# Turning the keys and the probabilities of a decode attention on VectorE instead of TensorE

## The chip, the cores and the metric

The kernel runs on one core of a Trainium2 chip. The metric is the device time of one execution in microseconds (us), as the median of several runs. A core has TensorE (PE), whose matmuls read SBUF and write PSUM; VectorE (DVE), ScalarE (ACT) and GpSimd (POOL); SyncE (SP), which here issues nearly all the transfers; and 16 DMA engines that carry them. Each engine works through its own instructions in order and waits on semaphores for the others.

## The reference

One token `x` of 576 values goes through two branches, which a gate mixes:

```
q = (x @ wq)                       # 32 query heads of 128, wq is 576 x 4096
k, v = the last 4096 positions of the caches of 16 key heads, two query heads share one
p = softmax(q k^T / sqrt(128));  a = (p v) @ wo        # wo is 4096 x 576
h = gelu(x @ w1 + b1);           b = h @ w2 + b2       # w1 576 x 4608, w2 4608 x 576
g = sigmoid(sum(x * gate_w));    out = g * a + (1 - g) * b
```

All tensors are bf16. Keys and values are 16.8 MB each, the four weight matrices 20.1 MB together; every byte is used once, 53.6 MB in all.

## The kernel before

The 16 key heads are taken four at a time (`HT`), so there are four key tiles and four value tiles (`NT`), each 128 partitions of 32 KB, 4.19 MB. Partition `p` of a tile belongs to head `p // 32` of the four and holds 128 consecutive positions of 128 values (`load_kv`, L104). The pool `kv_pool` has three buffers that keys, values and at the end `w2` pass through in turn; `w_pool` has two for `wq`, `w1` and `wo`. All these loads are issued by SP, in the order of the program text, and a load waits until the last reader of its buffer is done; what stands behind it on SP waits too. The order of the transfers is: first quarter of `wq`, k0, the rest of `wq`, k1, k2, v0, the first half of `w1`, k3, the second half of `w1`, v1, v2, v3, `wo` in two halves, `w2` in eight pieces.

The schedule is manual: on every engine the instructions run in the order in which the text issues them, and the framework adds the waits.

Scores need the keys with their 128 values on the partitions. `transposes(h, i)` (L276) makes four matmuls of 128x128 with `perm`, a permuted identity, as moving operand (L281), into one PSUM tile `tp`, and then copies it to `kT` as bf16, three of eight on DVE (L290), five on ACT (L292). `UT` is 4, so a key tile is worked in four units of eight such steps; `kT_pool` has four buffers.

`scores(h, s)` (L302) makes four matmuls of 32 columns of output partitions each, which PE runs side by side (L311). `qz` holds the queries between zeros; a window into it (`lo`) places two query columns at the row pair that belongs to the unit, so that the scores of two tiles gather in one PSUM bank `s_ps`, batch by batch (`TB` is 2, `NB` is 2).

`softmax(b)` (L319) copies the scores to SBUF, takes row maxima, turns these on PE to one row, joins the rows of a head, spreads the result back and takes the exponential on ACT with the sum accumulated (L355). `put(n)` (L363), four for each batch, turns the probabilities on PE (L367), and DVE multiplies them with a mask into `ez` (L374). `values(h, i)` (L391) multiplies `ez` with the value tile, 32 matmuls a tile in four column groups (L400), and `heads_out(t)` (L414) adds up the four masked blocks on DVE and turns the result on PE (L430).

`w1_mul` (L498) is the first layer of the other branch, `gelu` (L517) adds the bias, turns `h` with nine steps on PE (L538) and evaluates the gelu into `gt`. `gate` (L580) and `norm` (L598) make the mixing factor and the softmax scale. At the end `ow` (L733), the scaled attention in column form, is multiplied with `wo` in blocks of four rows (L759), the same loop goes on over the first rows of `w2`, and `part_s` (L766) gathers these sums. The last rows of `w2` are added in `row_matmul` (L776), then the result is copied and stored.

The main loop (L633) interleaves these: for each unit of keys the eight steps of the next unit, the two score steps, one step of the softmax `chain`, later the value matmuls of the first tile and the first layer. After it the value matmuls of the second tile stand between the steps of the second softmax, and the nine turns of `h` between its `put`s.

Of the kernel before, what the change touches and what calls it, by code (L numbers as in the profile page):

```python
# [16 lines left out]
def kernel(  # L17
# [28 lines left out]
    UT = 4  # L46
    NCH = NCK // UT
    NU = NT * UT
    F = 4608
# [22 lines left out]
    NBL = NCH // BC  # L72
    NBK = 2 * UT
    CB = NCK // NBK
    QZ = 2 * (TB * NBK - 1)

# [3 lines left out]
    w_pool = ctx.enter_context(tc.tile_pool(name="w_pool", bufs=2))  # L80
    const = ctx.enter_context(tc.tile_pool(name="const", bufs=1))
    kT_pool = ctx.enter_context(tc.tile_pool(name="kT_pool", bufs=4))
    small = ctx.enter_context(tc.tile_pool(name="small", bufs=1))
    ps_t = ctx.enter_context(tc.tile_pool(name="ps_t", bufs=3, space=bass.MemoryType.PSUM))
    ps_s = ctx.enter_context(tc.tile_pool(name="ps_s", bufs=1, space=bass.MemoryType.PSUM))
    ps_m = ctx.enter_context(tc.tile_pool(name="ps_m", bufs=1, space=bass.MemoryType.PSUM))
    ps_o = ctx.enter_context(tc.tile_pool(name="ps_o", bufs=1, space=bass.MemoryType.PSUM))
# [30 lines left out]
    WMAX = 41 * 256  # L118

    def load_flat(src, lo, n, name, cuts=(), between=None):  # L120
        t = w_pool.tile([P, WMAX], BF16, name=name, tag="w")
        edges = (0, *cuts, n)
        for i, (a, b) in enumerate(zip(edges, edges[1:])):
            if i == 1 and between is not None:
                between()
            nc.sync.dma_start(out=t[:, a:b], in_=src[:, lo + a : lo + b])  # L126
        return t
# [15 lines left out]
    def first_keys():  # L143
# [5 lines left out]
    QP = 2 * NM  # L149
    wq_t = [  # L150
        load_flat(wq_flat, 0, QP * QC, "wq_t", (NQ * QC,), first_keys),
        load_flat(wq_flat, QP * QC, QP * QC, "wq_t"),
    ]

# [17 lines left out]
    qz = const.tile([P, Hkv, QZ + 34], BF16, name="qz")  # L172
# [45 lines left out]
    for t in range(TB):  # L218
        nc.vector.tensor_reduce(
            out=m_b[:, t, 0:R].rearrange("p (g q) -> p g q", q=2),  # L220
            in_=ident_f[:].rearrange("p (g t b q) -> p t g q b", g=HT, t=TB, q=2)[:, t],
            axis=AX.X,
            op=ALU.add,
        )
    nc.vector.tensor_scalar(
        out=m_b[:].rearrange("p t x -> p (t x)"), in0=m_b[:].rearrange("p t x -> p (t x)"),
        scalar1=1.0 / HT, scalar2=None, op0=ALU.mult,
    )
    own = const.tile([P, HT], FP32, name="own")
    nc.vector.tensor_reduce(  # L230
        out=own[:], in_=ident_f[:].rearrange("p (i g) -> p g i", g=HT), axis=AX.X, op=ALU.add
    )
    own_r = const.tile([P, R], FP32, name="own_r")
    nc.vector.tensor_copy(
        out=own_r[:].rearrange("p (g q) -> p g q", q=2),
        in_=own[:].rearrange("p (g o) -> p g o", o=1).to_broadcast([P, HT, 2]),
    )
    perm = const.tile([P, P], BF16, name="perm")
    nc.vector.tensor_copy(
        out=perm[:].rearrange("p (g i) -> p g i", g=HT),  # L240
        in_=ident[:].rearrange("p (i g) -> p g i", g=HT),
    )
    pick = const.tile([P, TB * NBK, HT, 2], BF16, name="pick")
    nc.vector.tensor_copy(
        out=pick[:], in_=ident[:].rearrange("p (g x q) -> p x g q", g=HT, q=2)
# [30 lines left out]
    def transposes(h, i):  # L276
        if i == 0:
            kT[h] = kT_pool.tile([P, W], BF16, name="kT", tag="kT")
        tp = ps_t.tile([P, BC * P], FP32, name="tp", tag="tp")
        for c in range(BC):  # L280
            nc.tensor.matmul(  # L281
                tp[:, c * P : (c + 1) * P],
                lhsT=k_tiles[h // UT][:, (h % UT) * NCH + i * BC + c, :],
                rhs=perm[:],
                start=True,
                stop=True,
            )
        dst = kT[h][:, i * BC * P : (i + 1) * BC * P]
        if i in (0, 3, 6):
            nc.vector.tensor_copy(out=dst, in_=tp[:])  # L290
        else:
            nc.scalar.copy(out=dst, in_=tp[:])  # L292


    s_tiles = {}


    NN = CB // BC
    ez = const.tile([P, TB, NBK, NN, BC, R], BF16, name="ez")
    sums = const.tile([P, NB], FP32, name="sums")  # L300

    def scores(h, s):  # L302

        t, b = h // UT, 2 * (h % UT) + s
        row = NBK * (t % TB) + b
        if row == 0:
            s_tiles[t // TB] = ps_s.tile([P, CB, PI], FP32, name="s_ps", tag="s")
        lo = QZ - 2 * row
        kT_v = kT[h][:].rearrange("p (c g i) -> p c g i", g=HT, i=PI)
        for g in range(HT):  # L310
            nc.tensor.matmul(  # L311
                s_tiles[t // TB][32 * g : 32 * (g + 1), :, :],
                lhsT=qz[:, HT * t + g, lo : lo + 32],
                rhs=kT_v[:, s * CB : (s + 1) * CB, g, :],
                start=(row == 0),
                stop=(row == TB * NBK - 1),
            )

    def softmax(b):  # L319
# [3 lines left out]
        ms = small.tile([P, CB, PI], FP32, name="ms", tag="ms")  # L323
        m16 = small.tile([1, HT * TB, 2], FP32, name="m16", tag="m16")
        m_all = small.tile([1, P], FP32, name="m_all", tag="m_all")
        nb = small.tile([P, 1], FP32, name="nb", tag="nb")
        pr = small.tile([P, CB, PI, HT], BF16, name="pr", tag="pr")

        def row_max():
            nc.vector.tensor_copy(out=ms[:], in_=s_ps[:])  # L330
            nc.vector.tensor_reduce(  # L331
                out=mx[:], in_=ms[:].rearrange("p c i -> p (c i)"), axis=AX.X, op=ALU.max
            )

        def turn_max():
            mT = ps_m.tile([1, P], FP32, name="mT", tag="m")
            nc.tensor.transpose(out=mT[:], in_=mx[:], identity=ident_f[:])
            nc.vector.tensor_reduce(
                out=m16[:], in_=mT[:].rearrange("o (a b q) -> o a q b", b=NBK, q=2), axis=AX.X,
                op=ALU.max,  # L340
            )
            nc.vector.tensor_copy(
                out=m_all[:].rearrange("o (a b q) -> o a b q", b=NBK, q=2),
                in_=m16[:].rearrange("o a (b q) -> o a b q", b=1).to_broadcast(
                    [1, HT * TB, NBK, 2]
                ),
            )

        def spread():
            mb = ps_m.tile([P, 1], FP32, name="mb", tag="m")  # L350
            nc.tensor.matmul(mb[:], lhsT=m_all[:], rhs=ones_ff[0:1, 0:1], start=True, stop=True)
            nc.vector.tensor_scalar(  # L352
                out=nb[:], in0=mb[:], scalar1=-SCALE, scalar2=None, op0=ALU.mult
            )
            nc.scalar.activation(  # L355
                out=pr[:].rearrange("p c i g -> p (c i) g"),
                in_=ms[:].rearrange("p c (i g) -> p (c i) g", g=1).to_broadcast(
                    [P, CB * PI, HT]
                ),
                func=ACT.Exp, bias=nb[:, 0:1], scale=SCALE, accum_out=sums[:, b : b + 1],  # L360
            )

        def put(n):  # L363
            pool, tag = (ps_m, "m") if b == 0 else (ps_t, "tp")
# [268 lines left out]
    for h in range(UT - 1, NU):  # L633
# [27 lines left out]
        if h == UT + 2:  # L661
            gate()
# [164 lines left out]
```

## Time and profile before

| what | value |
|---|---|
| median of 3 runs | 134.89 us (134.27 to 136.29) |
| the profiled execution's own time | 133.93 us |
| its span, first to last instruction | 132.1 us |
| mean granted TensorE clock | 0.88 |
| PE, DVE, ACT busy | 90.1, 62.4, 50.3 us |
| DMA queue q1 | 53.62 MB, 95.4% of 16 engines' span |
| instructions | 2599, of them 1121 matmuls |

The profiled execution has about 1.8 us outside its span. Busy time of an engine is the time in which it has an instruction in work; several matmuls can be in work at once, so a group's busy time is less than its count times the mean of one. In groups of instructions a line reads: line of the kernel, engine, operation, output and inputs with shapes, count, then busy us, mean ns of one, and the idle time of the engine ahead of them with what ended it.

### The profile page before, as it was taken

To read this page: it belongs to the slowest core of one execution; us is meant where nothing else is said; L and a number is where in the kernel's file an instruction comes from. 1 tells how busy PE (TensorE), PEld (TensorE's weight loads), DVE (VectorE), ACT (ScalarE), POOL (GpSimd) and SP (SyncE) were. 2 spreads that over 40 slices of the span, in tenths; PEclk is the share of its full clock that TensorE was granted. 3 is DMA by queue.
4 is the path that set the end of the run, shared out by engine and by line. 5 is a ranking of instruction groups with operands and counts; after the bars stand their busy time and mean duration, and the time that the engine had idled before them with its cause. 6 is when DMAs were issued, how large, how long until landed. Compare 5 with 4: busy or idle time off the path is not lost.

```text
span 132.1 us, 2599 instructions
## 1 busy us (share of the span) xinstructions
PE 90.1 (68%) x1121; PEld 59.5 (45%) x1121; DVE 62.4 (47%) x144; ACT 50.3 (38%) x89; POOL 2.9 (2%) x10
## 2 busy tenths in 40 slices
PE   0000578896698879497889998984799655472562
PEld 0000577663465656266655575751496321241241
DVE  2910255662255546836535457487376475400021
ACT  3000256980277777483475646580600000000001
POOL 8000000000000000000000000000000000000000
PEclk9999999999999999955599999999965777779855
DMA  4998999999899999999989999999999899999960
GB/s 112 514 417 387 408 460 441 436 461 440 367 476 451 407 407 426 427 426 466 446 365 439 470 441 387 456 441 407 436 456 432 386 435 430 414 416 414 429 247 0
DMA packets 3448, 53.77 MB, mean 407 GB/s; under 512 B 483, under 2 KB 750, under 8 KB 1390
## 3 DMA queue, kind: packets, MB, share of 16 engines
q1 hardware_dynamic: 3434, 53.62, 95.4%
q8 instruction: 8, 0.13, 0.4%
q14 instruction: 2, 0.02, 0.0%
q10 hardware_dynamic: 4, 0.00, 0.0%
HBM read 53.62 MB, written 0.00 MB: 406 GB/s over the span
## 4 chain that ended last, share of the span: by engine, by line
DMA 40%; PE 32%; DVE 14%; issue 5%; ACT 5%; SPq 2%; DVEq 0%; ACTq 0%
DMA k_t<-in_A_k_cache_dram 22%; DMA w_t<-in_B_w_dram 18%; PE tp L281 12%; DVE kT L290 7%; PE acc L400 4%; PE s_ps L311 4%; ACT kT L292 3%; PE pT L367 3%; PE hT L538 3%; PE h_ps L507 2%; DVE ez L374 2%; ACT pr L355 2%; SPq L126 1%; DVE h_r L526 1%; DVE mx L331 1%
## 5 line engine op out<-in xcount | busy, mean ns | idle before, releaser
L281 PE MATMUL tp<-perm,k_t 128*128 128x128 bf16 x512 | 45.0, 236 | 20.2 <-DMA k_t<-in_A_k_cache_dram 15.5
L292 ACT CAST kT<-tp 128x512 bf16<-128x512 f32 x80 | 44.0, 587 | 38.4 <-PE tp L281 37.0
L290 DVE CAST kT<-tp 128x512 bf16<-128x512 f32 x48 | 32.5, 689 | 35.7 <-PE tp L281 32.6
L281 PEld LDWEIGHTS <-k_t 128*128 128x128 bf16 x512 | 34.8, 106 | 31.8 <-DMA k_t<-in_A_k_cache_dram 15.9
L311 PE MATMUL s_ps<-kT,qz 128*32 128x512 bf16 x128 | 12.6, 409 | 1.2 <-DVE kT L290 0.9
L400 PE MATMUL acc<-v_t,ez 128*32 128x512 bf16 x128 | 12.9, 491 | 0.6 <-DMA v_t<-in_A_v_cache_dram 0.6
L795 ACT CAST y<-y_ps 1x144 bf16<-1x144 f32 x2 | 0.5, 270 | 27.4 <-PE y_ps L778 27.4
L374 DVE TENSOR_TENSOR ez<-pT,own_r 128x512 bf16<-128x512 f32 x8 | 5.5, 690 | 3.2 <-PE pT L367 3.0
L759 PE MATMUL part<-w_t,gt 128*1 128x288 bf16 x46 | 2.9, 315 | 4.7 <-DMA w_t<-in_B_w_dram 4.7
L767 DVE SCALAR_TENSOR_TENSOR part_s<-b_r,omg,part 128x576 f32<-128x576 bf16 x1 | 0.8, 812 | 11.0 <-PE part L759 11.0
L355 ACT ACTIVATE pr<-ms,nb 128x2048 bf16<-128x2048 f32 x2 | 4.0, 2002 | 4.7 <-DVE nb L352 4.7
L400 PEld LDWEIGHTS <-ez 128*32 128x32 bf16 x128 | 3.9, 114 | 4.2 <-issue 3.1
L311 PEld LDWEIGHTS <-qz 128*32 128x32 bf16 x128 | 3.6, 94 | 4.7 <-DVE kT L290 1.2
L367 PE MATMUL pT<-pick,pr 128*128 128x128 bf16 x32 | 4.3, 281 | 1.8 <-DVE ez L374 1.1
L367 PEld LDWEIGHTS <-pr 128*128 128x128 bf16 x32 | 3.5, 144 | 3.2 <-ACT pr L355 1.6
L538 PEld LDWEIGHTS hT<-sel_f,h_r 128*128 128x128 f32 x18 | 4.7, 332 | 0.4 <-DVE nb L352 0.4
L538 PE MATMUL hT<-sel_f,h_r 128*128 128x8 f32 x18 | 4.9, 375 | 0.0
L422 DVE SCALAR_TENSOR_TENSOR a_s<-acc,m_c,a_s 128x128 f32<-128x128 f32 x12 | 4.2, 350 | 0.4
L759 PE MATMUL part<-wo_t,ow 128*1 128x288 bf16 x64 | 3.5, 392 | 1.1 <-DVE ow L735 1.1
L759 PEld LDWEIGHTS <-gt 128*1 128x1 bf16 x46 | 1.5, 83 | 5.8 <-issue 5.3
L430 PE MATMUL o_ps<-a_s,m_r 128*32 128x128 f32 x8 | 1.8, 317 | 3.0 <-DVE a_s L422 2.9
L430 PEld LDWEIGHTS o_ps<-a_s,m_r 128*32 128x32 f32 x8 | 0.8, 126 | 5.1 <-DVE a_s L422 4.6
(91 smaller groups left out, 46.3 us busy)
## 6 DMA issues: line engine op xcount, KB each, us to landing
k_t<-in_A_k_cache_dram SPq DMA_DIRECT2D x4, 4096.0 KB, 30.0
v_t<-in_A_v_cache_dram SPq DMA_DIRECT2D x4, 4096.0 KB, 25.4
w_t<-in_B_w_dram SPq DMA_DIRECT2D x2, 2592.0 KB
wo_t<-in_A_wo_dram SPq DMA_DIRECT2D x2, 2304.0 KB, 24.4
w_t<-in_B_w_dram SPq DMA_DIRECT2D x2, 1296.0 KB, 27.7
wq_t<-in_A_wq_dram SPq DMA_DIRECT2D x1, 2304.0 KB
wq_t<-in_A_wq_dram SPq DMA_DIRECT2D x1, 1792.0 KB, 16.2
w_t<-in_B_w_dram SPq DMA_DIRECT2D x1, 864.0 KB
```

The costliest lines, as they stand in the source:

```text
L281: nc.tensor.matmul(tp[:, c * P : (c + 1) * P], lhsT=k_tiles[h // UT][:, (h % UT) * NCH + i * BC + c, :], rhs=perm[:], start=True, stop=True,)
L290: nc.vector.tensor_copy(out=dst, in_=tp[:])
L292: nc.scalar.copy(out=dst, in_=tp[:])
L311: nc.tensor.matmul(s_tiles[t // TB][32 * g : 32 * (g + 1), :, :], lhsT=qz[:, HT * t + g, lo : lo + 32], rhs=kT_v[:, s * CB : (s + 1) * CB, ...
L355: nc.scalar.activation(out=pr[:].rearrange("p c i g -> p (c i) g"), in_=ms[:].rearrange("p c (i g) -> p (c i) g", g=1).to_broadcast([P, CB ...
L367: nc.tensor.matmul(pT[:, c, :, :].rearrange("p x r -> p (x r)"), lhsT=pr[:, n * BC + c, :, :].rearrange("p i g -> p (i g)"), rhs=pick[:].r ...
L374: nc.vector.tensor_tensor(out=ez[:, :, :, n, :, :].rearrange("p t b c r -> p c (t b) r"), in0=pT[:], in1=own_r[:].rearrange("p (a b r) -> ...
L400: nc.tensor.matmul(acc[t][32 * ct : 32 * ct + BC * R, :, :], lhsT=ez[:, t % TB, n // NN, n % NN, :, :].rearrange("p c r -> p (c r)"), rhs= ...
L422: nc.vector.scalar_tensor_tensor(out=a_s[:], in0=acc[t][:, c, :], scalar=m_c[:, c : c + 1], in1=a_s[:], op0=ALU.mult, op1=ALU.add,)
L507: nc.tensor.matmul(h_box[0][32 * t : 32 * (t + 1), k, 0:FB], lhsT=x2[:, m, :], rhs=w[:, off : off + FB], start=(m == 0), stop=(m == NM - 1),)
L538: nc.tensor.matmul(box[0][:, j, :, :].rearrange("p e g -> p (e g)"), lhsT=rows[:, j : j + RJ * (P - 1) + 1 : RJ], rhs=sel_f[:].rearrange(" ...
L759: nc.tensor.matmul(part[32 * t : 32 * t + 1, k, 0:DB], lhsT=col, rhs=w[:, i * D + k * DB : i * D + (k + 1) * DB], start=(n == 0), stop=(n ...
```

## The change

Keys are turned by DVE. Two bf16 values are taken as one 32-bit word; `transposes(h)` is two `nc.vector.transpose` of 128x2048 words, which turn each block of 32 partitions by 32 words in itself, from the key tile straight to `kT` in SBUF, with no matmul and no PSUM. `UT` is 2: a key tile is two units `h` of 64 positions for each partition, and `kT_pool` has two buffers. Since a block is turned only inside its 32 partitions, a quarter of `kT`'s partitions holds one of the four position groups (`NA`), and a word's two halves and the two halves of the 128 values give four products (`NBP`) to be added up.

The query is therefore laid out block-diagonally in `qz` (33 blocks of 128 columns, refilled for each batch by `queries(b)`: four copies, one for each 32 partitions), and `scores(h)` makes 16 matmuls of 128 output partitions and 512 columns, which gather all rows of a batch in one bank; their moving operand steps over words (two bf16 values 4 bytes apart, then 32 bytes on). `q_r` is spread by four pairs of copies, alternately on DVE and ACT, and turned by 16 small matmuls.

The softmax reads the scores from PSUM, without the copy to SBUF; one exponential for each of the four heads, with a bias that is -1e30 for rows of the other heads, replaces the mask (`off`), and one DVE transpose for each batch (`turn`) turns the probabilities to `ez`, with no `put`s. `ez` has one part for each batch.

`w_pool` has one buffer of double size: `wq`, then `w1` in one load, then `wo`. In the text of the program `w1` now comes behind k3. The interleaving is gone: the steps are written one after the other. `own`, `own_r`, `perm` and `pick` go, `ps_s`, `ps_m` and `ps_o` have two buffers each, and the `tp` bank triple goes.

```diff
-    UT = 4
+    UT = 2
+    NA = 4
+    PQ = PI // NA
+    ND = Dh // 2
+    NBP = 4
+    QW = P
...
-    w_pool = ctx.enter_context(tc.tile_pool(name="w_pool", bufs=2))
+    w_pool = ctx.enter_context(tc.tile_pool(name="w_pool", bufs=1))
-    kT_pool = ctx.enter_context(tc.tile_pool(name="kT_pool", bufs=4))
+    kT_pool = ctx.enter_context(tc.tile_pool(name="kT_pool", bufs=2))
...
+    def transposes(h):
+        k = k_tiles[h // UT][:].rearrange("p c d -> p (c d)")
+        kT[h] = kT_pool.tile([P, NCH * ND], FP32, name="kT", tag="kT")
+        n = NCH * ND // 2
+        for i in range(2):
+            lo = (h % UT) * NCH * Dh + i * 2 * n
+            nc.vector.transpose(
+                out=kT[h][:, i * n : (i + 1) * n].rearrange("p (x e l) -> p x l e", e=HT, l=2),
+                in_=k[:, lo : lo + 2 * n].bitcast(FP32),
+            )
...
+    def scores(h):
+        t, ch = h // UT, h % UT
+        b, tt = t // TB, t % TB
+        if h % (TB * UT) == 0:
+            s_tiles[b] = ps_s.tile([P, NCH, PQ], FP32, name="s_ps", tag="s")
+        kT_v = kT[h][:].bitcast(BF16).rearrange(
+            "p (c b i e l o) -> p c b i e l o", b=2, i=PQ // 2, e=HT, l=2, o=2
+        )
         for g in range(HT):
+            for bp in range(NBP):
+                r = (((g % 2) * NBP + bp) * 2 + g // 2) * TB + tt
+                lo = r * QW + QX - (16 * tt + R * ch + 2 * g)
+                nc.tensor.matmul(
+                    s_tiles[b][:].rearrange("p c (i l) -> p c i l", l=2),
+                    lhsT=qz[:, lo : lo + P],
+                    rhs=kT_v[:, :, bp // 2, :, g, :, bp % 2],
...
+            nc.vector.scalar_tensor_tensor(
+                out=nb[:], in0=mb[:].to_broadcast([P, HT]), scalar=-SCALE, in1=off[:],
+                op0=ALU.mult, op1=ALU.add,
+            )
+            for g in range(HT):
+                nc.scalar.activation(
+                    out=pr[:, :, g], in_=s_ps[:].rearrange("p c i -> p (c i)"),
+                    func=ACT.Exp, bias=nb[:, g : g + 1], scale=SCALE,
+                    accum_out=sums[:, b, g : g + 1],
                 )
...
+        def turn():
+            nc.vector.transpose(
+                out=ez[:, b].rearrange("p x c r -> p c x r"),
+                in_=pr[:].rearrange("p x g -> p (x g)"),
+            )
...
+    def queries(b):
+        for a in range(NA):
+            rows = slice(PI * a, PI * (a + 1))
+            lo = QX + PI * a
+            nc.vector.tensor_copy(
+                out=qz[rows, lo : lo + NR * QW].rearrange(
+                    "p (e x t w) -> p e x t w", e=2, t=TB, w=QW
+                )[:, :, :, :, 0:2],
...
+    transposes(2)
+    scores(0)
+    scores(1)
+    transposes(3)
+    k_tiles[3] = load_k(3)
+    w1_t = load_flat(w1_flat, "w1_t")
+    gate_rows()
+    scores(2)
+    scores(3)
+    row_max, turn_max, spread, turn = softmax(0)
+    queries(1)
+    row_max()
+    turn_max()
+    spread()
+    transposes(4)
+    turn()
+    transposes(5)
+    v_tiles[1] = load_v(1)
+    gate()
+    scores(4)
+    scores(5)
+    values(0)
     v_tiles[2] = load_v(2)
+    for f in heads_out(0):
+        f()
+    transposes(6)
+    transposes(7)
     v_tiles[3] = load_v(3)
+    scores(6)
+    scores(7)
+    row_max, turn_max, spread, turn = softmax(1)
     row_max()
     turn_max()
     spread()
+    turn()
+
+    w1_mul(w1_t)
...
+    for f in gelu():
         f()
+    sums_start()
+    values(1)
+    for f in heads_out(1):
+        f()
+    values(2)
     norm()
+    for f in heads_out(2):
+        f()
+    values(3)
...
+    for f in heads_out(3):
+        f()
```

## The prediction

> **What bounds the kernel now.** I read the page's engine sums and slices first, then the DMA queues, then three stretches cut out of the slices, then single rows.
>
> ```profile
> span 132.1 us, 2599 instructions
> ...
> PE 90.1 (68%) x1121; PEld 59.5 (45%) x1121; DVE 62.4 (47%) x144; ACT 50.3 (38%) x89; POOL 2.9 (2%) x10
> ...
> PEclk9999999999999999955599999999965777779855
> DMA  4998999999899999999989999999999899999960
> ...
> q1 hardware_dynamic: 3434, 53.62, 95.4%
> ```
>
> No compute engine is over 68% busy, while the DMA row shows 9 in nearly every slice and the one data queue fills 95.4% of the span. The stream of 53.62 MB sets the time: k0 has landed at 14.5 us, the last piece of w2 at 128.1, and 48.9 MB in 113.6 us is 430 GB/s without a hole. The rest is about 1.5 us before the stream and 4 us after it. The change moves the same bytes and leaves the last matmuls as they are, so I find no gain over 2% to be had (2.7 us, about what a measurement of this kernel can tell from no change). What it can do is make the stream wait, or finish the computing later than the stream. The timeline of the stream's end shows how near that is:
>
> ```profile
> 112.39 0.41 PE L430 MATMUL o_ps<-a_s,m_r 128*32 128x128 f32 x2 [1.61 <-DVE a_s L422]
> 113.25 0.27 PE L725 MATMUL ow_ps<-ot,spread_o 128*128 128x128 bf16 x2 [0.45 <-DVE ot L409]
> 114.65 3.50 PE L759 MATMUL part<-wo_t,ow 128*1 128x288 bf16 x64 [1.13 <-DVE ow L735]
> 119.75 0.90 PE L759 MATMUL part<-w_t,gt 128*1 128x288 bf16 x18 [1.60 <-DMA w_t<-in_B_w_dram]
> ...
> 124.61 1.12 PE L759 MATMUL part<-w_t,gt 128*1 128x288 bf16 x10 [0.85 <-DMA w_t<-in_B_w_dram]
> ```
>
> After the attention's result (ow, ready at 114.6) PE waits for pieces of w2 three times. Those waits, 4.7 us together, are the slack: ow may come nearly 5 us later before the end moves.
>
> **What is removed.** 512 transposing matmuls (45.0 us of PE) with 128 evictions (44.0 us ACT, 32.5 DVE), and the 32 matmuls and 8 masked copies that turned the probabilities. All of it lies beside the stream and is worth nothing by itself. Setup edits end long before their users: qz is four times larger, its clearing at L173 grows from 0.95 to some 3.9 us on POOL and is done by about 8 us, first needed at 31; the mask tables on DVE become fewer.
>
> **Key transposes.** 16 DVE instructions of 128x2048 32-bit words, two for each half tile. The trace has no transpose, so I take the cost by element from the row of a read of like kind:
>
> ```profile
> L331 DVE TENSOR_REDUCE mx<-ms 128x1 f32<-128x512 f32 x2 | 1.4, 686 | 0.1
> ...
> L230 DVE TENSOR_REDUCE own<-ident_f 128x4 f32<-128x128 f32 x1 | 0.4, 368 | 0.0
> ...
> L191 DVE TENSOR_REDUCE par<-ident_f 128x1 f32<-128x64 f32 x2 | 0.3, 201 | 0.0
> ...
> L249 DVE TENSOR_REDUCE m_c<-ident_f 128x4 f32<-128x128 f32 x1 | 0.3, 275 | 0.0
> ```
>
> 686 ns for 512 and 275 for 128 contiguous words are 1.07 ns a word, so 2.3 us for 2048; evictions that follow each other start 0.09 us before the end of the one ahead, which leaves 2.25. The new instruction writes words 8 bytes apart. Steps cost something here: L230 steps 16 bytes and takes 93 ns more than L249 for the same 128 words, 0.73 ns a word. L191 steps 8 bytes and takes 201 ns for 64 words, where 275 less 64 x 1.07 is 207: no surcharge. I take 2.25 us, the nearest row in the step; the upper end is the 16-byte price, 2.25 + 2048 x 0.73 ns = 3.75 us. The lower end is half the price a word, 1.2 us (copies of 2-byte values, L202, take 208 ns for 128, less than L249). A half tile is then 4.6 us, a tile 9.2, against 9.75 us in which the stream brings 4.19 MB.
>
> **Scores.** Before, four matmuls of 32 columns ran side by side (36 such of wq, nine rounds, 2.1 us: 0.23 a round of 512). Now each is 128 wide and alone: 16 a half tile, 16 x 0.22 = 3.6 us at the full clock, 6.9 us at the half clock, whose price these stretches show:
>
> ```profile
> 50.00:56.00 6.00, 3.72 (x48) 2.52 (x45) 4.62 (x10) 3.74 (x7) 0.00 (x0) 1.00 0.90 380
> 56.00:66.00 10.00, 8.90 (x70) 6.45 (x70) 5.33 (x9) 5.17 (x9) 0.00 (x0) 0.50 1.05 454
> 66.00:76.00 10.00, 9.66 (x138) 5.54 (x140) 4.73 (x8) 6.93 (x13) 0.00 (x0) 0.99 1.00 428
> ```
>
> (PE busy is the first number after the length, the granted clock the third last.) After a stretch with PE idle for 2 us the clock was 0.50 for 10 us, though PE was 89% busy; score matmuls took 608 ns instead of 390. [...] PE will now idle while DVE turns keys, so I take 6.5 us for a half tile after a long pause and 3.6 for one that follows closely. The moving operand is read in pairs of 2-byte values 4 bytes apart, which no row shows; the lower end is 3.6, the upper 6.9 or more.
>
> **Softmax and probabilities.** From the row maximum to the exponential 2.3 us before, plus one more copy (0.2) and four query copies ahead of it in batch 0 (0.9). Four exponentials of 512 at 0.59 (an ACT eviction) plus 0.19 (accumulator read) are 3.1 us against 2.2. The turn to ez is one DVE instruction of 2048: 2.25 instead of four eviction rounds (59.2 to 64.5 in the timeline). With two key buffers each transpose also waits for the scores two halves back; behind it on DVE stand the softmax, the copies of the sums and the gelu.
>
> **The sum**, in us from the span's start. k0 lands 14.5, turned at 24.3 (v0 is asked for there, 29.1 before). wq, 8.9 MB into the stream, at 24.2. Then nine query rounds on a cold PE (2.1 at full clock, 3.9 at half: 3.5), two small copies on DVE and ACT each after the other (0.69 was one of 512 elements: 1.5 for both steps), 16 small matmuls with their loads (0.13 each: 2.0) and four copies into qz (1.0): 32.2. Scores 0: 38.7, and only now may the second tile's transposes write: 43.3, 47.9. So k3 is asked for at 47.9 (48.3 before). Scores 3: 51.5; queries and maximum: 55.1; transposes 4: 59.7; turn 62.0; transposes 5: 66.6, v1 asked for (71.4 before, and not needed until w1 has landed at 75.6). Scores 5 at 70.2, values 0 (2.4, between 1.8 and 3.6 by clock) 72.6, its sums 75.0, transposes 6 and 7: 84.2, v3 asked for, needed at 95. Scores 7 (6.5 + 3.6 from 79.6): 89.7; exponentials 95.4, turn 97.7. Then in series what was interleaved before: h_r 1.45 (L526), nine turns of h 4.2 (two took 0.90), gelu and clearing 3.0 (100.5 to 102.9, and L620): 106.3; sums of head group 1 (1.5) and their turn 0.45: 108.3; values 2: 110.7; norm and sums 113.9; values 3: 116.3; sums and ow 3.6: **119.9**, 5.3 us later than before. wo blocks 3.6, w2 blocks 2.9, part_s 0.85: 127.2; 2.8 for the last rows, 2.65 to the end: **132.7**. w2's first three blocks are asked for at 105.7, when values 1 have freed their buffer, and needed at 115.8. On SP each request waits behind the one ahead of it (w1 behind k3, wo behind v3), and still every one stands 5 us or more ahead of its need (k3 least: v0 has landed at 53.5), so the stream has no hole; of the 5.3 us the slack hides all but 0.6. The profiled execution took 133.93 us with its 132.1 of span, so it would be 134.5; the median of the runs shown stands 0.96 above the profiled one, and I forecast **135.5 us**. One weight buffer costs nothing: wq is used up at 28 us and w1 asked for at 47.9; w1 is used up at 95, wo needed at 104.9.
>
> **Rivals.** (1) **Scores set the pace**: if a half tile takes over 4.6 us (a transpose pair) each time, because the clock stays at half or the spaced reads cost double, DVE waits for PE. With 6.9 throughout, scores 3 end at 59.8, scores 5 at 81.8, scores 7 at 105, ow at 135; the span is 148, the time about 151. Against: the clock was 0.99 from 66 on under dense work. For: PE idles over 4 us at least three times. Half-way, 5.2 for each close half tile and 6.9 for the others, gives 139.5 of span, 142 us. (2) **Transposes at the 16-byte price**, 3.75 us: the second tile is turned at 56.5, so the stream waits 5 us for k3, 4 for v1 and 4 for v3, and the span is 154, the time 157; 154 if the probabilities' turn, which writes runs of 16 bytes, keeps its 2.25. Its point is 2.5 us an instruction; beyond, each 0.1 us adds 1.4 us. [...] (3) **The stream alone counts**: if cold half tiles are shorter, everything ends in the slack: 134.9, inside my forecast. (4) **Faster**: the stream would have to run 2% better; its dips (380 GB/s in 50 to 56) add up to about 1.3 us. Not enough.
>
> **How the numbers follow.** Forecast 0.49 (its own range 133.7 to 137.6); rival 1 with its half-way cases 0.31; rival 2 0.17; faster 0.03. So faster 0.03, same 0.49, slower 0.48. The range goes from 133.7 (no delay, dips gone) to 152, over rival 1 whole and the part of rival 2 between 2.5 and 3.5 us an instruction.
>
> **What would show it.** Right: DMA row at 9 to the end, transposes of 2.2 to 2.4 us, ow between 116 and 122, PE waiting for w2 at most twice. Wrong: transposes near 3.6; score matmuls spaced 0.43 at a granted clock of 1.0 (reads) or 0.5 (clock); holes in the DMA row before v1, v3 or wo.

## The result, and the profile after

| | before | after |
|---|---|---|
| median | 134.58 us (133.79 to 136.29, 4 runs) | 150.14 us (148.96 to 151.55, 4 runs) |
| profiled execution, its span | 133.93, 132.1 us | 150.89, 149.1 us |
| ow ready | 114.6 us | 138.3 us |

The ratio is 1.115, with a 95% interval from 1.101 to 1.129: the change makes the kernel some 15.5 us slower. Here and below, medians are over all executions of a kernel, while ratios and their intervals leave out the executions that fell into a slower state of the chip. The likeliest case of the prediction, 135.5 us, did not come; its first rival, "Scores set the pace", with 151 us, did.

From the page of the changed kernel, the lines that answer to those shown of before: the span, the busy times, the granted clock with the DMA share and rate in 40 slices of 3.73 us, the data queue, and the shares of the chain that ended last.

```profile
span 149.1 us, 1426 instructions
...
PE 90.7 (61%) x589; PEld 34.4 (23%) x589; DVE 68.3 (46%) x112; ACT 13.3 (9%) x25; POOL 5.6 (4%) x10
...
PEclk9999999999999999555999975899995555768599
DMA  5999999999999999998989999999369955999000
GB/s 177 474 431 431 448 431 422 422 425 422 422 422 426 442 360 422 459 490 378 389 315 422 422 413 422 422 413 431 154 183 430 435 218 178 424 411 402 17 0 0
...
q1 hardware_dynamic: 3146, 53.62, 86.0%
...
PE 54%; DVE 19%; DMA 14%; ACT 7%; issue 2%; SPq 1%; DVEq 0%; ACTq 0%
```

The same 53.62 MB no longer fill the span. Four slices (104 to 112 us and 119 to 127 us) run at 154 to 218 GB/s; against 422 they lose 4 x 3.73 us x (1 - 183/422) = 8.4 us, 183 being their mean. The stream is over at about 138 us, and the remaining 11 us (before: 4) are computing. PE is as busy as before (90.7 against 90.1 us) though 532 of its 1121 matmuls are gone, and 54% of the last chain are PE. The groups of the page name the instructions (busy us, mean ns of one, idle time ahead of them and what ended it):

```profile
L289 PE MATMUL s_ps<-kT,qz 128*128 128x512 bf16 x128 | 55.9, 608 | 10.5 <-DVE kT L266 9.0
L266 DVE STREAM_TRANSPOSE kT<-k_t 128x2048 f32<-128x2048 f32 x16 | 35.8, 2281 | 14.5 <-PE s_ps L289 9.6
...
L334 ACT ACTIVATE pr<-s_ps,nb 128x512 bf16<-128x512 f32 x8 | 9.9, 1404 | 72.0 <-DVE nb L329 72.0
...
L341 DVE STREAM_TRANSPOSE ez<-pr 128x2048 bf16<-128x2048 bf16 x2 | 4.6, 2312 | 5.8 <-ACT pr L334 5.1
```

128 score matmuls keep PE busy for 55.9 us. The first two lines wait for each other: PE idles 9.0 us for `kT` from DVE, and DVE 9.6 us for PE to give `kT`'s buffer back. The transposes take 2.28 us, as estimated; the exponentials (1404 ns) and the score matmuls do not.

The timeline of PE, runs of one group joined (start and length in us, and what ended the idle time before):

```profile
31.04 27.79 PE L289 MATMUL s_ps<-kT,qz 128*128 128x512 bf16 x64 [1.14 <-DVE qz L456]
...
66.92 7.07 PE L289 MATMUL s_ps<-kT,qz 128*128 128x512 bf16 x16 [4.24 <-DVE kT L266]
74.29 7.07 PE L289 MATMUL s_ps<-kT,qz 128*128 128x512 bf16 x16 [0.31 <-DVE ge L564]
...
90.07 13.97 PE L289 MATMUL s_ps<-kT,qz 128*128 128x512 bf16 x32 [4.78 <-DVE kT L266]
...
138.29 3.77 PE L706 MATMUL part<-wo_t,ow 128*1 128x288 bf16 x64 [1.13 <-DVE ow L682]
141.84 2.21 PE L706 MATMUL part<-w_t,gt 128*1 128x288 bf16 x46
```

Sixty-four score matmuls without a gap take 27.79 us, 0.434 us each; a half tile of 16 that stands alone takes 7.07. At the end PE waits for `ow` alone; the waits for `w2` are gone. Two windows cut out of such runs tell which of the two causes in the rival is at work (PE busy with its count first, granted clock third from the end):

```profile
51.00:55.00 4.00, 4.00 (x11) 1.02 (x9) 0.00 (x0) 0.00 (x0) 0.00 (x0) 1.00 1.03 401
66.90:70.00 3.10, 3.08 (x8) 0.92 (x8) 2.46 (x2) 0.60 (x3) 0.00 (x0) 0.50 1.05 455
```

At a granted clock of 1.00 eleven matmuls touch a window of 4.0 us, at 0.50 eight touch one of 3.1: the pace is the same. So it is not the clock. Nor is it DVE, ACT or POOL at work beside PE: in the first window they do nothing (the entries of 0.00), in the second DVE is busy for 2.46 us. That is what the prediction named for the spaced reads: "score matmuls spaced 0.43 at a granted clock of 1.0".

DVE's timeline shows what the pace does to the order of the work:

```profile
38.15 4.50 DVE L266 STREAM_TRANSPOSE kT<-k_t 128x2048 f32<-128x2048 f32 x2 [7.17 <-PE s_ps L289]
45.06 4.50 DVE L266 STREAM_TRANSPOSE kT<-k_t 128x2048 f32<-128x2048 f32 x2 [2.40 <-PE s_ps L289]
...
58.87 0.92 DVE L456 CAST qz<-q_ps 32x64 bf16<-32x64 f32 x4 [9.17 <-PE s_ps L289]
```

DVE stands still for 9.17 us up to 58.87: after transposes 3 and a step of the gate (0.2 us) its next work in the text is `queries(1)`, which refills `qz` and must wait until scores 3 have read it. Transposes 4, which need nothing but free `kT` buffers and k2, stand behind it. The same happens before transposes 6, which stand behind `heads_out(0)`.

### The profile page after: what moved, and what is told of

It reads as the page before. It is cut to its first block, busy times and chain, and to the rows that moved or that the text cites. A ratio compares the mean times of both kernels' runs of the same rounds, so it can differ in the third digit from the quotient of the medians.

```text
span 149.1 us, 1426 instructions
## 1 busy us (share of the span) xinstructions
PE 90.7 (61%) x589; PEld 34.4 (23%) x589; DVE 68.3 (46%) x112; ACT 13.3 (9%) x25; POOL 5.6 (4%) x10
## 3 DMA queue, kind: packets, MB, share of 16 engines
q1 hardware_dynamic: 3146, 53.62, 86.0%
HBM read 53.62 MB, written 0.00 MB: 360 GB/s over the span
## 4 chain that ended last, share of the span: by engine, by line
PE 54%; DVE 19%; DMA 14%; ACT 7%; issue 2%; SPq 1%; DVEq 0%; ACTq 0%
PE s_ps L289 33%; DMA wq_t<-in_A_wq_dram 14%; PE acc L360 8%; ACT pr L334 7%; DVE kT L266 6%; PE part L706 4%; DVE ez L341 3%; PE hT L508 3%; DVE a_s L382 3%; PE q_ps L419 2%; DVE qz L456 1%; PE o_ps L390 1%; DVE h_r L496 1%; DVE mx L307 1%; DVE a_s L378 1%
## 5 line engine op out<-in xcount | busy, mean ns | idle before, releaser
L289 PE MATMUL s_ps<-kT,qz 128*128 128x512 bf16 x128 | 55.9, 608 | 10.5 <-DVE kT L266 9.0
L266 DVE STREAM_TRANSPOSE kT<-k_t 128x2048 f32<-128x2048 f32 x16 | 35.8, 2281 | 14.5 <-PE s_ps L289 9.6
L289 PEld LDWEIGHTS <-qz 128*128 128x128 bf16 x128 | 14.6, 115 | 49.4 <-issue 48.1
L334 ACT ACTIVATE pr<-s_ps,nb 128x512 bf16<-128x512 f32 x8 | 9.9, 1404 | 72.0 <-DVE nb L329 72.0
L419 PE MATMUL q_ps<-wq_t,x 128*32 128x512 bf16 x36 | 4.2, 627 | 8.8 <-DVE x L411 4.7
L403 PE MATMUL x_ps<-x,dup 64*128 64x9 bf16 x1 | 0.2, 165 | 14.3 <-DMA x<-in_A_x_dram 14.3
L341 DVE STREAM_TRANSPOSE ez<-pr 128x2048 bf16<-128x2048 bf16 x2 | 4.6, 2312 | 5.8 <-ACT pr L334 5.1
L456 DVE CAST qz<-q_ps 32x64 bf16<-32x64 f32 x8 | 1.8, 221 | 10.5 <-PE s_ps L289 9.2
L419 PEld LDWEIGHTS <-x 128*32 128x32 bf16 x36 | 1.5, 134 | 18.4 <-issue 18.3
L170 DVE CAST ident_f<-ident 128x128 f32<-128x128 bf16 x1 | 3.9, 3879 | 2.4 <-POOL ident masks.py:199 2.4
L173 POOL MEMSET qz<- 128x4224 bf16 x1 | 3.6, 3617 | 0.0
```

The costliest lines, as they stand in the source:

```text
L170: nc.vector.tensor_copy(out=ident_f[:], in_=ident[:])
L173: nc.gpsimd.memset(qz[:], 0.0)
L266: nc.vector.transpose(out=kT[h][:, i * n : (i + 1) * n].rearrange("p (x e l) -> p x l e", e=HT, l=2), in_=k[:, lo : lo + 2 * n].bitcast(FP32),
L289: nc.tensor.matmul(s_tiles[b][:].rearrange("p c (i l) -> p c i l", l=2), lhsT=qz[:, lo : lo + P], rhs=kT_v[:, :, bp // 2, :, g, :, bp % 2] ...
L334: nc.scalar.activation(out=pr[:, :, g], in_=s_ps[:].rearrange("p c i -> p (c i)"), func=ACT.Exp, bias=nb[:, g : g + 1], scale=SCALE, accum ...
L341: nc.vector.transpose(out=ez[:, b].rearrange("p x c r -> p c x r"), in_=pr[:].rearrange("p x g -> p (x g)"),)
```

## Experiments

### The columns that PE reads

Three kernels change only which columns of `kT` a score matmul reads, at the same count of 512; transposes, loads and order stay. The first takes 512 adjacent values:

```diff
-                    rhs=kT_v[:, :, bp // 2, :, g, :, bp % 2],
+                    rhs=kT[h][:].bitcast(BF16)[:, (NBP * g + bp) * 512 : (NBP * g + bp + 1) * 512],
```

> The changed kernel, but each of the 16 score matmuls of a half tile reads 512 adjacent 2-byte values of kT instead of the values of its own head and part, so the scores are sums of wrong products; counts, shapes and order stay. Theory (the spaced read costs double): matmuls follow each other in 0.22 us where the granted clock is 1.0 and in 0.43 where it is 0.5, the first half tile after a pause takes 5 to 6.5 us, the next 3.6; scores 7 end near 90 us instead of 104, span 133 to 138, time 135 to 140. Rival (the width of 128 output columns or the weight load sets 0.43): spacing stays 0.43, time 149 to 152.

Measured: 133.82 us, ratio 0.9996 (0.9979 to 1.0012). The page's group, then PE's timeline:

```profile
L289 PE MATMUL s_ps<-kT,qz 128*128 128x512 bf16 x128 | 34.8, 436 | 9.0 <-DVE kT L266 7.6
```

```profile
45.94 1.89 PE L289 MATMUL s_ps<-kT,qz 128*128 128x512 bf16 x8 [0.31 <-DVE kT L266]
...
119.42 0.90 PE L706 MATMUL part<-w_t,gt 128*1 128x288 bf16 x18 [1.36 <-DMA w_t<-in_B_w_dram]
122.51 1.59 PE L706 MATMUL part<-w_t,gt 128*1 128x288 bf16 x18 [2.20 <-DMA w_t<-in_B_w_dram]
```

Eight matmuls take 1.89 us, 0.215 us apart after the first one's latency. The busy time of the group falls by 21.1 us, ow is ready at 113.9 us, PE waits for `w2` again, and all the loss is gone. It is gone although the exponentials still take 1.41 us and the order is unchanged, so the pace of the score matmuls alone is enough to explain the loss. The expectation's rival, the 128 output columns or the weight load, is out, since both are as in the change. The second kernel takes every second value of an unbroken run of 1024, a step of 4 bytes without a jump:

```diff
-                    rhs=kT_v[:, :, bp // 2, :, g, :, bp % 2],
+                    rhs=kT[h][:].bitcast(BF16).rearrange("p (y x o) -> p y x o", y=8, o=2)[:, (NBP * g + bp) // 2, :, bp % 2],
```

> As e1_run, but each score matmul reads every second 2-byte value of one unbroken run of 1024, a step of 4 bytes with no jump; the scores are again sums of wrong products. If the step of 4 bytes between neighbours is the price (one 4-byte word a column): spacing 0.43, time 149 to 152. If only the jump of 32 bytes to another place costs: spacing 0.22, time 135 to 140.

Measured: 133.62 us, ratio 0.9986 (0.9958 to 1.0014).

```profile
L289 PE MATMUL s_ps<-kT,qz 128*128 128x512 bf16 x128 | 36.3, 448 | 7.1 <-DVE kT L266 5.8
```

```profile
60.30 1.97 PE L289 MATMUL s_ps<-kT,qz 128*128 128x512 bf16 x8 [0.95 <-DVE kT L266]
```

The step of 4 bytes is nearly free: eight matmuls take 1.97 us instead of 1.89, some 0.226 us apart. The third takes two adjacent values and then jumps, as the changed kernel does, by 32 bytes:

```diff
-                    rhs=kT_v[:, :, bp // 2, :, g, :, bp % 2],
+                    rhs=kT_v[:, :, bp // 2, :, g, bp % 2, :],
```

> As e1_run, but each score matmul reads two adjacent 2-byte values, then jumps 32 bytes on (the roles of the word's halves and of the neighbouring positions are exchanged, so the scores are sums of wrong products). If the step inside a pair is the price: spacing 0.22, time 135 to 140, since a whole 4-byte word is used. If the jump is the price: spacing 0.43, time 149 to 152.

Measured: 150.79 us, ratio 1.124 (1.118 to 1.130).

```profile
L289 PE MATMUL s_ps<-kT,qz 128*128 128x512 bf16 x128 | 55.9, 608 | 10.5 <-DVE kT L266 9.0
```

The line is that of the changed kernel, digit for digit. The price is neither in the step between the two values nor in reading halves of words, but comes with going on to another place after every two columns: 0.434 us a matmul, against 0.226 without the jump.

### Longer runs before the jump

If two columns before a jump are too few, four or eight may do. DVE's write can lay `kT` out that way: it then writes 32-bit words 16 (or 32) bytes apart instead of 8.

```diff
-                out=kT[h][:, i * n : (i + 1) * n].rearrange("p (x e l) -> p x l e", e=HT, l=2),
+                out=kT[h][:, i * n : (i + 1) * n].rearrange("p (x e l) -> p x l e", e=HT, l=4),
...
-            "p (c b i e l o) -> p c b i e l o", b=2, i=PQ // 2, e=HT, l=2, o=2
+            "p (c b i e l o) -> p c b i e l o", b=2, i=PQ // 4, e=HT, l=4, o=2
```

> The changed kernel with runs of 4 positions of one head in kT instead of 2: a score matmul reads 4 values 4 bytes apart (16 bytes in all), then jumps; the key transposes write words 16 bytes apart instead of 8. Theory for PE (each jump costs about 0.86 ns, (0.43 - 0.21) us over 256 jumps): half the jumps, 0.32 us a matmul; if only runs that leave a 16-byte piece half read cost, 0.22. For DVE: the surcharge of a 16-byte step that reads show, 0.73 ns a word, holds for writes too: 3.7 us a transpose instead of 2.28; if writes are free, 2.28. With both theories time 153 to 160; with free writes 134 to 142.

> As e5_l4 with runs of 8: PE reads 8 values 4 bytes apart, then jumps 224 bytes on; the transposes write words 32 bytes apart. PE by the price of a jump: 0.27 us a matmul; by the half-read piece: 0.22. DVE: 3.7 us a transpose, as for 16 bytes, or more if the price grows with the step. Time 152 to 158; with free writes 134 to 138.

Measured with runs of four: 149.74 and 154.95 us; with runs of eight: 152.51 and 155.28 us. Two executions each are too few for an interval, but neither is near 134. From the page of the kernel with runs of four:

```profile
GB/s 175 437 443 417 425 443 443 443 419 453 425 434 419 430 18 425 425 463 359 538 359 266 434 434 425 425 284 142 443 430 338 404 434 280 435 406 419 128 0 0
...
L266 DVE STREAM_TRANSPOSE kT<-k_t 128x2048 f32<-128x2048 f32 x16 | 59.0, 3779 | 11.6 <-PE s_ps L289 6.4
L289 PE MATMUL s_ps<-kT,qz 128*128 128x512 bf16 x128 | 37.7, 459 | 27.1 <-DVE kT L266 22.2
```

Four columns before the jump bring the full rate back: a half tile takes 3.62 us at the full clock (3.63 with runs of eight), and the group's busy time is 37.7 instead of 55.9 us. (So the expectation's first theory, 0.86 ns added for each jump and 0.32 us a matmul, fell.) But a transpose now takes 3.78 us instead of 2.28. DVE sets the pace in PE's stead, PE waits 22.2 us for `kT`, and the stream stands almost still (18 GB/s) in the slice from 52 to 55 us, where k3 is late. So the cost has moved, not gone: this is the prediction's second rival, brought about by the layout, and its price for a transpose was right (3.75 us in the text, 3.78 on the chip). In those two layouts what is cheap for PE's read is dear for DVE's write.

### The exponentials

They write each fourth 16-bit value of `pr`, since the four heads lie interleaved. Here each head has its own stretch, and the turn reads with the step instead:

```diff
-        pr = small.tile([P, NCH * PQ, HT], BF16, name="pr", tag="big")
+        pr = small.tile([P, HT, NCH * PQ], BF16, name="pr", tag="big")
...
-                    out=pr[:, :, g], in_=s_ps[:].rearrange("p c i -> p (c i)"),
+                    out=pr[:, g, :], in_=s_ps[:].rearrange("p c i -> p (c i)"),
...
-                in_=pr[:].rearrange("p x g -> p (x g)"),
+                in_=pr[:].rearrange("p g x -> p x g"),
```

> The changed kernel with the probabilities stored head by head: each exponential writes 512 adjacent values instead of every fourth, and the DVE turn of the probabilities reads 4 runs 1 KB apart instead of one. Theory (the step of the write is what makes an exponential 1.18 us apart instead of 0.78): exponentials 0.65 to 0.8 us apart, a softmax 1.5 to 2.1 us shorter there; the turn takes 2.3 (jumps free) to 3.8 us (0.73 ns a word more); time 0 to 4 us less, 146 to 150. Rival (the PSUM source or the accumulator sets the price): 1.18 stays, time 150 to 153.

Measured: 149.46 us, ratio 1.116 (1.111 to 1.120); the span is 147.8 us, 1.3 less than that of the change.

```profile
L334 ACT ACTIVATE pr<-s_ps,nb 128x512 bf16<-128x512 f32 x8 | 5.4, 686 | 74.9 <-DVE nb L329 74.9
...
L341 DVE STREAM_TRANSPOSE ez<-pr 128x2048 bf16<-128x2048 bf16 x2 | 7.4, 3686 | 2.9 <-ACT pr L334 2.9
```

An exponential falls from 1404 to 686 ns: the write at steps of 8 bytes had doubled it. DVE's turn rises from 2.31 to 3.69 us in exchange. The four exponentials of a batch take 2.78 us instead of 4.95, so 2.2 us are won against 1.4 lost; but in batch 0 transposes 4 had hidden nearly all of the exponentials, and only the loss is left there. From the start of the row maximum to the end of the turn, batch 0 takes 10.6 us instead of 10.05 and batch 1 takes 9.2 instead of 9.8: together no gain. Most of the 1.3 us of span come from elsewhere. This is the main part of values 2 on PE, in the change and then in this run:

```profile
125.60 3.25 PE L360 MATMUL acc<-v_t,ez 128*32 128x512 bf16 x29
```

```profile
125.57 1.89 PE L360 MATMUL acc<-v_t,ez 128*32 128x512 bf16 x29
```

The granted clock in these stretches was 0.58 in the change's profiled execution; in this one the page's slice from 125.6 to 129.3 us has 0.9 or more. The ratios to the kernel before are the same, too (1.115 and 1.116). So the doubled write is a second cost of the change, but this layout only hands it on to DVE, and no run shows what it is worth at the end.

### The order of the steps

The instructions are those of the change, with their costs; only their order in the text differs, and `h_r` has a buffer of its own so that it needn't wait for the turn. Transposes 4 go ahead of the refilling of `qz`, the scores of the second batch between the steps of the first softmax, and the first layer ahead of scores 7:

```diff
     row_max, turn_max, spread, turn = softmax(0)
+    transposes(4)
     queries(1)
     row_max()
+    scores(4)
+    transposes(5)
+    v_tiles[1] = load_v(1)
     turn_max()
     spread()
+    scores(5)
+    transposes(6)
     turn()
...
     scores(6)
-    scores(7)
...
     w1_mul(w1_t)
...
+    scores(7)
```

> The changed kernel with the same instructions in another order and h_r in a buffer of its own: transposes 4 ahead of the second queries, transposes 5 and 6 and scores 4 and 5 between the steps of the first softmax, the first layer of the other branch and the turns of h beside the last scores and the second exponentials. The spaced reads stay, 0.43 us a matmul. Theory (the price of the reads reaches the end only because PE and DVE wait for each other in series): scores run nearly without pause from 31 us, scores 7 end at 92 to 96 instead of 104, values 1 start at 104 to 107 instead of 120, span 132 to 136, time 134 to 138. Rival (56 us of scores on PE are too much in any order): less than 5 us gained, time 145 or more.

Measured: 134.98 us, ratio 1.0077 (1.0033 to 1.0122). From the page, and from PE's timeline:

```profile
L289 PE MATMUL s_ps<-kT,qz 128*128 128x512 bf16 x128 | 56.1, 608 | 2.1 <-DVE qz L456 2.1
```

```profile
86.81 7.07 PE L289 MATMUL s_ps<-kT,qz 128*128 128x512 bf16 x16
...
121.79 4.00 PE L709 MATMUL part<-wo_t,ow 128*1 128x288 bf16 x64 [1.13 <-DVE ow L685]
```

The score matmuls are as slow as in the change (7.07 us a half tile), but PE waits 2.1 us for DVE instead of 10.5, the last scores end at 93.9 us instead of 104.0, and 14.5 of the 15.5 us are back. So the loss has two conditions: the doubled price of the read, and an order in which PE and DVE wait for each other. Undoing the first brings back all of it, undoing the second all but 1.0 us. This order also moves the first layer, and with it the request for `wo`, ahead of scores 7; no run takes these moves apart. The remaining 1.0 us (0.4 to 1.6) has its place too: `wo`'s blocks start at 121.8 us, 7.1 later than before, which is more than the slack of 4.7 us that PE's waits for `w2` made up.

Both remedies that keep the transposes cheap, the order and `pr` by heads:

> e7_order together with the adjacent writes of e4_exp. If e7_order ends above the stream's 132 us of span, this takes another 1 to 2 us off; if e7_order already ends with the stream, the two are the same within 0.3%, 133.5 to 135 us, and neither is below the kernel before.

Measured: 135.66 us, ratio 1.004 (0.999 to 1.009): no different from the order alone, nor from before. The 1 to 2 us that the expectation hoped for do not show; here too the turn takes 3.69 us.

### A layout that is cheap for both

The transposes can write words in adjacent pairs, if two neighbouring partitions hold rows of one head. (In the key tiles partition p belongs to head p mod 4 of the four, in both kernels; the section on the kernel before says p // 32, which is wrong. The steps and durations used so far do not depend on it.) Here partition p holds head (p // 2) mod 4. Runs of four columns for PE, pairs for DVE and pairs for the exponentials follow from it. Here each tile is loaded in two parts, one for the even and one for the odd partitions:

```diff
+            "e (i l c) d -> l i e (c d)", l=2, c=NCK
...
+        for l in range(2):
+            nc.sync.dma_start(out=t[l : P - 1 + l : 2], in_=rows[l])
...
-                out=kT[h][:, i * n : (i + 1) * n].rearrange("p (x e l) -> p x l e", e=HT, l=2),
+                out=kT[h][:, i * n : (i + 1) * n].rearrange("p (x e j l) -> p x j e l", e=HT, j=2, l=2),
...
-                    out=pr[:, :, g], in_=s_ps[:].rearrange("p c i -> p (c i)"),
+                    out=pr[:, :, g, :], in_=s_ps[:].rearrange("p c (i l) -> p (c i) l", l=2),
```

> The text of the changed kernel with the keys laid so that two neighbouring partitions hold rows of one head (each key tile comes in two loads, one for the even and one for the odd partitions). The transposes then write words in adjacent pairs, the score matmuls read four neighbouring values of 16 bits before each jump, and the exponentials write pairs of values. Theory (a run of four is read at the full rate, and the writes of DVE stay cheap in pairs): score matmuls 0.215 us apart at the full clock (0.43 in the changed kernel), a half tile 3.6 instead of 7.07 us; transposes 2.28 us as in the changed kernel; time 133.3 to 134.8 us, equal to the kernel before. Rival A, the jump of DVE's write decides and not its run: transposes near 3.7 us, time 149 to 155 as with the layout of four neighbouring rows before. Rival B, the loads suffer, since each touches only every second partition: the stream falls under 420 GB/s and the time is over 137 us even with short scores and transposes. Exponentials, 1.40 us in the changed kernel for single values at steps of 8 bytes: 0.7 if a pair is enough, 1.4 if it is the jump.

> The kernel of the run before this one (neighbouring partitions hold rows of one head) with the order of steps in which PE and DVE work past each other. Theory: both remedies bring the time to the stream's and do not add up, 133.0 to 134.8 us, no gain over the kernel before, with the last result of the attention (ow) several us earlier and PE waiting for w2 at the end. If transposes cost 3.7 us (rival A): 16 of them are 60 us of DVE, the reads of scores are short, and the order hides a part: 136 to 145 us. If the loads suffer (rival B): the same time as the run before this one, over 137 us.

Measured: 213.24 us (212.19 to 214.22), ratio 1.586 (1.573 to 1.599); with the other order 214.41 us (210.69 to 223.90, four executions). The page of the first:

```profile
GB/s 199 243 231 212 305 405 299 199 231 232 225 212 196 212 255 220 206 206 206 249 244 386 402 307 212 209 249 224 199 215 249 230 199 199 287 424 420 417 379 14
...
L265 DVE STREAM_TRANSPOSE kT<-k_t 128x2048 f32<-128x2048 f32 x16 | 35.8, 2283 | 45.0 <-DMA k_t<-in_A_k_cache_dram 45.0
L288 PE MATMUL s_ps<-kT,qz 128*128 128x512 bf16 x128 | 34.7, 435 | 37.2 <-DVE kT L265 34.8
...
L333 ACT ACTIVATE pr<-s_ps,nb 128x512 bf16<-128x512 f32 x8 | 5.6, 724 | 84.8 <-DVE nb L328 84.8
```

On the engines all came as the theory had it: the score matmuls have the busy time of adjacent reads (34.7 us), the transposes stay at 2.28 us and an exponential takes 724 ns. But keys and values now come at some 210 GB/s, while the weights at the end, on all partitions, still come at 420: rival B. DVE waits 45.0 us for keys. I then tried whether an even and an odd load side by side fill the stream, the odd ones issued by POOL:

```diff
-            nc.sync.dma_start(out=t[l : P - 1 + l : 2], in_=rows[l])
+            (nc.sync, nc.gpsimd)[l].dma_start(out=t[l : P - 1 + l : 2], in_=rows[l])
```

> The kernel with neighbouring rows of one head in neighbouring partitions (e9), with the loads of the even partitions issued by SP and those of the odd ones by POOL, so that both can run at once. In e9 every load of 2.1 MB that touches each second partition ran at some 210 GB/s, half of the 430 of a load on all partitions, while score matmuls (0.215 us apart) and transposes (2.28 us) were as wanted. Theory: the half rate comes from the set of partitions that one load touches, and an even and an odd load at once bring 400 GB/s or more; then the time is 133.5 to 138 us. Rival: rows of every second partition go at half rate whatever runs beside them; then some 200 to 215 us, as e9.

> The same with the order of steps in which PE and DVE work past each other. Theory: if the stream is back at over 420 GB/s, 133.0 to 137 us, the same as the run before this one within 2 us, since neither score matmuls nor transposes are then on the path; no gain over the kernel before, whose stream is the same. Rival (half rate stays): 200 to 215 us.

Measured: 223.90 us, ratio 1.672 (1.659 to 1.685), and 224.55 us, ratio 1.642 (1.625 to 1.658). My theory fell, and both times lie even above the rival's 200 to 215 us. In the page of the first the two queues have their shares:

```profile
q1 hardware_dynamic: 2634, 36.85, 62.5%
q0 software_dynamic: 640, 16.78, 33.9%
```

Together they are busy for 96% of the 16 DMA engines' span and yet the mean is 242 GB/s (before: 95.4% and 407). The 16.78 MB of the odd loads, POOL's queue, keep the engines busy for 33.9% of 222.0 us, 75 us; before, as many bytes took 39 us by the share of q1, so the packets take 1.9 times as long. A second queue adds nothing: the span is 222.0 us against 210.4. Why the packets take longer is not shown: no run has a load onto 64 partitions that lie side by side, or two loads that do not alternate. Whether a layout by pairs of rows can be loaded in one piece is left open; no run here has one, so none shows the three prices at their low end with a full stream.

## Where the prediction failed and where it held

The likeliest case missed: it had 135.5 us, within 133.7 to 137.6, and 150.14 were measured. The whole range, 133.7 to 152, holds the result only because it was drawn over the first rival, and the result lies near its upper end; so it does not speak for the sum. What came true is that rival, which had a chance of 0.31 and named the mechanism.

Step by step; the milestones are those of the sum, in us from the span's start.

| milestone | sum | measured | late |
|---|---|---|---|
| scores 0 begin | 32.2 | 31.0 | -1.2 |
| scores 0 done | 38.7 | 38.1 | -0.6 |
| k3 asked for (transposes 3 done) | 47.9 | 49.6 | 1.7 |
| scores 3 done | 51.5 | 58.8 | 7.3 |
| turn of batch 0 done | 62.0 | 69.9 | 7.9 |
| scores 5 done | 70.2 | 81.4 | 11.2 |
| scores 7 done | 89.7 | 104.0 | 14.3 |
| turn of batch 1 done | 97.7 | 113.9 | 16.2 |
| ow ready | 119.9 | 138.3 | 18.4 |
| end | 132.7 | 149.1 | 16.4 |

- **Scores: the step that failed.** The prediction took "6.5 us for a half tile after a long pause and 3.6 for one that follows closely". Half tiles took 6.95 to 7.07, which is the upper end ("6.9 or more") that the text gave and set aside. It had put its weight on the clock, for which rows existed, and left the spaced read, for which none did, at the cheap end. The lateness grows by 8.5 in the first four half tiles (from -1.2 to 7.3), by 3.3 between the first turn and the end of scores 5 and by 3.1 up to scores 7: 14.9 of the 19.6 us that it grows by until ow. (Another 2.2 come between the second turn and ow, mainly since the value matmuls of a tile took 3.4 to 3.6 us, put at 2.4, at granted clocks of 0.50 to 0.61.) The first kernel of the experiments changes only these reads and all of the loss goes; the second and third put the price on reads that jump after two columns.
- **Exponentials: a mis-sized term.** 3.1 us for four, from an eviction of 0.59 and an accumulator read of 0.19; measured 4.95, the write's step being left out of account. In batch 0 the transposes beside them hid nearly all of it; in batch 1 nothing did (the lateness grows by 1.9).
- **Key transposes: right**, and so was the upper end. (L249, which the text calls contiguous, reads runs of eight words; L262, with unbroken runs of 64, has the same 275 ns, so the price stands.) 2.25 us were taken, 2.28 measured, and a pair takes 4.50; 3.75 was the upper end for steps of 16 bytes, and the kernels that write at 16 bytes measured 3.78. The turn of the probabilities was put at 2.25 and took 2.31. No run shows the 3.5 us an instruction up to which the range took in rival 2: with words 8 bytes apart a transpose took 2.28 us, 1.11 ns a word, and with words 16 bytes apart 3.78, 1.85 ns a word.
- **"The stream has no hole": wrong.** The requests up to v3 came late within their reserve (k3 at 49.6, v1 at 74.2 against 66.6, v3 at about 94 against 84.2), but `wo` was asked for at 108.6 instead of 95, and `w2`'s first blocks at 123.5 instead of 105.7. Those are the thin slices at 104 to 112 and 119 to 127 us. The requests are 13.6 and 17.8 us late, about as late as the steps ahead of them in the table, so the holes follow from the half tiles.
- **Slack: right in kind.** ow 5 us later was said to cost little. With adjacent reads it was ready at 113.9 and cost nothing; in the other order it came 7.1 us later than before and cost 1.0 us. That first figure also shows the sum pessimistic by some 6 us where half tiles are short.
- **One weight buffer: right about the time, not about the stream.** The request for `wo` waits until the first layer has read `w1` out of that one buffer (SP waits 13.6 us for L477, until 108.6), which makes the first thin stretch. The trace shows no cost of it at the end, since `wo`'s blocks wait for `ow` alone.
- **Setup: right.** `qz`'s clearing (3.6 us on POOL) is over long before its first reader.
- **Rival 1: right in mechanism and size**: 6.9 us throughout was to give ow at 135, a span of 148 and 151 us; it gave 138.3, 149.1 and 150.9. That the end fits better than ow is luck: ow came 3.3 us later than that, and what follows it took 10.8 us instead of 13, with no wait for `w2`. Of the two causes that it joined, the runs leave the spaced reads. No run of this layout shows the 5.2 us for a close half tile of its half-way case: all eight took 6.95 to 7.07.

What the prediction did not see is that an order can hide even the doubled price: 56 us of score matmuls fit beside a stream of 128, and the sum laid them end to end with DVE's work because the text does.

## What to carry to other kernels

Where a layout is made by one engine and read by another, price the access pattern of both ends, and keep the expensive end when no row of the trace shows such a read: here half the rate of PE's moving operand was worth 15 us, while the step of 4 bytes alone (0.226 us a matmul instead of 0.215) cost nothing that shows in the time. Before the layout is blamed alone, see whether the two engines wait for each other in turn: here the idle time of each of two groups of instructions ended with the other's (9.0 us on PE, 9.6 on DVE), and another order brought 14.5 us back. And a layout is not chosen for the engines only: loads that each touched every second partition ran at half the rate, some 210 GB/s against 420.

## What was not expected of the hardware

- **PE's moving operand, 16-bit values**: 512 columns took some 0.215 us at the full clock when read adjacent (eight matmuls in 1.89 us), or in runs of four or eight at 4-byte steps before a jump (sixteen in 3.62 and 3.63), and 0.226 at steps of 4 bytes without a jump; they took 0.434 us in runs of two before a jump, at a granted clock of 1.00 and of 0.50 alike. At 0.50 seven matmuls on adjacent columns are in work in the 2.6 us from 71.4 to 74 us of the run with adjacent reads, so one takes at least 0.37 us and at most 0.43, and there the jumps cost at most 0.06 us. In numbers, 256 runs in 0.434 us are 1.7 ns a run, and 128 runs of four in 0.215 us are 1.7 ns as well; what sets this time is not shown.
- **ACT's write**: an exponential of 512 took 1404 ns when it wrote one 16-bit value every 8 bytes, 724 in pairs at steps of 16 bytes, and 686 adjacent.
- **DVE's transposes of 2048**: 2.28 us with 32-bit words written 8 bytes apart or in adjacent pairs, 3.78 at 16 and at 32 bytes; with 16-bit values 2.31 us from an adjacent read and 3.69 from one that jumps for each value.
- **Loads onto every second partition** ran at some 210 GB/s, half of the 420 on all 128, with the 16 DMA engines shown busy over 96% of the span, and a second queue did not help (a span of 222.0 us against 210.4).
